# Six low-word roundings go to VectorE, w_in's fourths are converted ahead of w_out's, and the issue order is ranked anew

## The chip, the cores and the metric

The kernel runs on one core of one Trainium2 chip. The metric is the device time in microseconds of one execution. The profile calls the engines PE (TensorE), DVE (VectorE), ACT (ScalarE), POOL (GpSimd) and SP (SyncE, which issues the transfers); PEld is TensorE's weight load.

## The reference, cut to what matters

Three stages follow one another. `x` is 8 x 8 x 512 x 64 and `state` 8 x 8 x 32 x 64; the mixture stages see 4352 tokens of 512 columns. The weights `w_in` and `w_out` reach the kernel as 64-bit floats, so each element is a low and a high 32-bit word.

```python
def attn(x, state):                        # both directions of attention
    a = softmax(scale * x @ state.T);  xread = a @ state
    a2 = softmax(scale * state @ x.T); sread = a2 @ x
    return concatenate([xread, sread], axis=2)
def moe(x, w_in, w_out):                   # 512 -> 2048 -> 512
    h = x @ w_in
    return (h * sigmoid(h)) @ w_out
def moe2(x, phi, w1, w2):                  # 32 slots, 8 experts
    logits = x @ phi
    slots = softmax(logits, axis=0).T @ x
    slot_out = per expert: relu(slots @ w1) @ w2
    return softmax(logits, axis=1) @ slot_out
```

## The kernel before

The tokens are worked through in nine blocks: blocks 0 to 7 hold the 512 read tokens of one batch entry each, block 8 the 256 state tokens. A block does the attention of its batch entry, then 16 hidden tiles `h` (`hid`, 128 hidden columns each): six full-array matmuls on split (high and low part) operands into one PSUM bank, an activation into a tile `g` (six buffers), a VectorE transpose into `blk`. The tiles of one fourth of the hidden columns use one product `wb` of the state with a fourth of `w_in`, made by `wb_mm` with tiled matmuls `wbp` and then split by a ScalarE copy (high part) and a VectorE or GpSimd subtraction (low part). `logits` multiplies `g` by `w2p`, which is w_out times phi, one fourth at a time; until it has run, the `g` buffers stay in use. `s_rep` and `s_dTg` are the softmax over tokens and the slot sums `S`.

Ahead of this, and beside block 0, the two 64-bit weights are turned into fp32. Each comes as four fourths in two halves, 16 halves of 1024 KB in all (`raw`). `conv` (line 546) does one half in four steps: ScalarE's Prelu pass on the high words (`win<-raw` or `acc<-raw` in the profile); ScalarE's Identity pass, which scales and rounds the low words to integers (`part<-raw,ulps`); VectorE's shift of the first result by 3 bits (`win<-win`, `acc<-acc`); GpSimd's integer addition of the two (`win<-win,part`, `acc<-acc,part`). The halves go in the order w_in, w_in, w_out, w_out for each fourth (line 532). A finished w_in fourth lets its `wbp` run; a finished w_out fourth goes through `w2ps` (matmul), a copy `w2s`, `w2q` (matmul) and a copy into `w2p`. Eight raw halves fit in two buffers; a later load is issued when a half has been converted. In blocks 1 to 6 `conv_nat` (line 556) converts w_out once more in another layout; its two-input VectorE operation `blk<-blk` reads the strided low words too.

In block 0 the softmax of the first batch entry stands in front of the first `h`: scores `sc` in PSUM, ScalarE's copy `e`, VectorE's transposes `s`, reductions (`tm`, `asm`), a subtraction, `a_soft1` to `a_soft3`, and the split `ar`, whose low part VectorE computes for this entry.

The order of the instructions on each engine is not that of the code. A recorder (`Recorder`, line 124) collects all operations; its `schedule` plays them through with a cost for each and picks, for the engine that can go first, the ready operation with the smallest rank. The rank is the operation's number in the code, plus `nc.shift`, plus an entry of the table `RANK` (line 48) by zone ("0" is block 0 and what stands ahead of it, "m" blocks 1 to 6, then "7" and "8"), engine, operation, name and count. `LOOK` is how far ahead in time an engine looks for a better candidate. `STAY` and `KEEP` say how much worse a rank may be so that TensorE goes on with full-array work (`STAY`) or tiled work (`KEEP`):

```python
near = [c for c in cands if (c[1].mode == FULL) == (mode == FULL)]
if near:
    near = min(near, key=lambda c: (c[1].prio + SAME * (change(c[1]) > 0.2), c[0]))
    if near[1].prio <= pick[1].prio + (STAY if mode == FULL else KEEP):
        pick = near
```

At the end stand the expert weights `w1` and `w2` (32 MB as loads from `in_w_dram` into `place`, `blk` and `acc`, each issued once its place is free), the slot products `sia`, `sib`, `f`, `so`, and the output tiles `o`.

All compute instructions are recorded on one line of the kernel (427, in `issue`), so the rows are told apart by their tiles.

Of the kernel before, what the change touches and what calls it, by code (L numbers as in the profile page):

```python
# [8 lines left out]
F32R = mybir.dt.float32r  # L9
U32 = mybir.dt.uint32  # L10
# [15 lines left out]

BY_PE = (NB,)

WIN = (2, 6)
WIN8 = (0, 2)  # L30

# [14 lines left out]


RANK = {
    ("0", "ACT", "activation", "acc", 0): 8,
    ("0", "ACT", "activation", "part", 12): 8,  # L50
    ("0", "ACT", "activation", "win", 3): 13,
    ("0", "ACT", "copy", "wb", 2): 71,
    ("0", "DVE", "tensor_scalar", "acc", 0): -9,
    ("0", "DVE", "tensor_scalar", "asm", 3): 120,
    ("0", "DVE", "tensor_tensor", "wb", 0): 459,
    ("0", "DVE", "tensor_tensor", "wb", 3): 126,
    ("0", "DVE", "transpose", "blk", 7): -36,
    ("0", "DVE", "transpose", "s", 4): -40,
    ("0", "PE", "matmul", "lg", 5): 58,
    ("0", "PE", "matmul", "lg", 7): -81,  # L60
    ("0", "PE", "matmul", "wq", 3): -125,
    ("0", "PE", "transpose", "eT", 2): 59,
    ("0", "PE", "transpose", "srT", 1): -75,
    ("7", "DVE", "tensor_reduce", "m", 0): 434,
    ("7", "PE", "matmul", "h", 0): -39,
    ("7", "PE", "matmul", "h", 8): -120,
    ("7", "PE", "matmul", "lg", 5): 30,
    ("7", "PE", "matmul", "wbp", 1): 76,
    ("8", "DVE", "scalar_tensor_tensor", "fin", 0): 68,
    ("8", "PE", "matmul", "S", 3): 155,  # L70
    ("8", "PE", "matmul", "f", 9): 165,
    ("8", "PE", "matmul", "f", 13): 120,
    ("8", "PE", "matmul", "h", 17): 166,
    ("8", "PE", "matmul", "lg", 6): 120,
    ("8", "PE", "matmul", "so", 4): 51,
    ("8", "PE", "transpose", "gt", 8): 71,
    ("8", "PE", "transpose", "hT", 3): -134,
    ("8", "PE", "transpose", "lT", 0): 120,
    ("m", "ACT", "activation", "m", 0): 698,
    ("m", "DVE", "tensor_scalar", "asm", 1): 28,  # L80
    ("m", "PE", "matmul", "S", 2): -150,
    ("m", "PE", "matmul", "h", 5): -324,
    ("m", "PE", "matmul", "lg", 8): -96,
    ("m", "PE", "matmul", "lg", 9): -50,
    ("m", "PE", "transpose", "lT", 0): 416,
}


# [35 lines left out]
class Recorder:  # L124
# [90 lines left out]
    def cost(self, op, eng, what, outs, ins, kwargs):  # L215

        def n(v):
            r = 1
            for s, c in list(v.ap)[1:]:
                r *= c  # L220
            return r

        ps = bass.MemoryType.PSUM
        most = max(n(v) for v in outs + ins)
        pin, pout = any(v.space == ps for v in ins), any(v.space == ps for v in outs)
        strided = any(list(v.ap)[-1][0] > 1 and list(v.ap)[-1][1] > 1 for v in outs + ins)
        if eng == PE:
            lhs, rhs = kwargs.get("lhsT"), kwargs.get("rhs")
            if what == "transpose":
                op.mode, op.tail = FULL, 0.2  # L230
                op.cost += 0.11
                return
            rows, cols = list(lhs.ap)[0][1], n(lhs)
            op.mode = (128 if rows > 64 else 64 if rows > 32 else 32, 128 if cols > 64 else 64 if cols > 32 else 32)
            N = n(rhs)
            if op.mode == FULL:
                split = rhs.dtype == F32R
                op.cost += N / 2.4e3 + 0.0212 if split else max(0.2, 4 * N / 2.4e3 + (0.021 if N > 256 else 0.04))
                op.tail = 0.165
            else:  # L240
                tiles = (128 // op.mode[0]) * (128 // op.mode[1])
                m = 2 * len(op.calls)
                op.cost = max(m / tiles * 2 * N / 2.4e3, m * 0.0135) + (0.07 if tiles == 16 else 0.0068 * tiles)
                op.tail = 0.165
        elif eng == ACT:
            f = kwargs.get("func")
            base = 0.833e-3 * most
            if f in (AF.Abs, AF.Sign, AF.Relu):
                lat = base + (0.26 if pin else 0.29)
            elif len(ins) > 1 and most < 1024:  # L250
                lat = base + (0.258 if pin else 0.285)
            else:
                lat = base + (0.16 if pin else 0.205)
            if kwargs.get("accum_out") is not None:
                op.cost, op.tail = lat + 0.096, 0.0
            else:
                op.cost, op.tail = lat - 0.105, 0.105
            op.mode = {AF.Exp: "e", AF.Silu: "s", AF.Tanh: "es"}.get(f)
        elif eng == DVE:
            sb = [kwargs[x] for x in ("in0", "in1") if x in kwargs and kwargs[x].space == bass.MemoryType.SB]  # L260
            fast = not pin and not pout and what in ("tensor_scalar", "tensor_copy")
            op.port = len(sb) > 1 or fast
            if what == "transpose":
                lat = 0.165 + most / 0.96e3
            elif what == "reciprocal":
                lat = 0.165 + max(0, most - 4) * 6.7e-3
            elif fast:
                lat = 0.262 + most / 1.92e3
            else:
                lat = (0.205 if pin and len(ins) > 2 else 0.155) + most / 0.96e3  # L270
            op.cost, op.tail = lat - 0.08, 0.0 if fast else 0.08
        elif eng == POOL:
            lat = 0.2 + most * 2.135e-3
            if most == 1024:
                lat = 2.39 if outs[0].dtype == F32R else 1.94
# [26 lines left out]
    def schedule(self):  # L302
# [37 lines left out]
        while n_left:  # L340
            best = None
            for e in avail:
# [110 lines left out]
        return lambda *a, **k: self._rec.record(self._eng, what, call, a, k)  # L453


LOOK = {PE: 0, DVE: 0.302, ACT: 0.098, POOL: 0.05, SP: 0.0}
DMA_RATE = 405e3
FULL = (128, 128)
STAY, KEEP, SAME = 60, 60, 30


@with_exitstack
def tile_state_attention_soft_moe(
# [91 lines left out]

# [21 lines left out]
    def share(half):  # L577
        return part[:, 2 * half:2 * half + 2]

    def wo_half(fq, half):  # L580

        n = 4 * fq + 2 + half
        conv(raw_at(n), acc[:, 2 * half:2 * half + 2], share(half))
        if n >= 4:
            next_raw()
        if half == 0:
# [11 lines left out]
        nc.scalar.mul(out=w2p[:, fq].rearrange("p i s -> p (i s)"), in_=p[:, 0:128], mul=-0.5)  # L598

    def win_half(fq, half):  # L600
        n = 4 * fq + half
        conv(raw_at(n), win_t[fq][:, :, 256 * half:256 * half + 256], share(half))
        if n >= 4:
            next_raw()

# [49 lines left out]
    def a_split(b):  # L655
# [506 lines left out]
    for k in range(NB):  # L1162
# [4 lines left out]
        for j in range(16):  # L1167
# [107 lines left out]
    p = s_dTg(NB)  # L1275
# [177 lines left out]
```

## Time and profile before

| what | us |
|---|---|
| median of 3 runs (467.29 to 468.88) | 467.94 |
| the profiled execution | 466.55 |
| its span | 464.0 |
| PE busy in the span | 414.1 (89%) |
| DVE busy | 296.3 (64%) |
| ACT busy | 279.6 (60%) |
| POOL busy | 135.5 (29%) |

The span runs from the first to the last instruction of the profiled execution; that execution's own time is 2.55 us longer. A row of the timeline gives start, duration, engine, operation, output and inputs, and in brackets how long the engine was idle before and what ended that. The chain of waits follows the end of the kernel back to what released it at each step.

### The profile page before, as it was taken

To read this page: it belongs to the slowest core of one execution; us is meant where nothing else is said; L and a number is where in the kernel's file an instruction comes from. 1 tells how busy PE (TensorE), PEld (TensorE's weight loads), DVE (VectorE), ACT (ScalarE), POOL (GpSimd) and SP (SyncE) were. 2 spreads that over 40 slices of the span, in tenths; PEclk is the share of its full clock that TensorE was granted. 3 is DMA by queue.
4 is the path that set the end of the run, shared out by engine and by line. 5 is a ranking of instruction groups with operands and counts; after the bars stand their busy time and mean duration, and the time that the engine had idled before them with its cause. 6 is when DMAs were issued, how large, how long until landed. Compare 5 with 4: busy or idle time off the path is not lost.

```text
span 464.0 us, 12243 instructions
## 1 busy us (share of the span) xinstructions
PE 414.1 (89%) x5334; PEld 261.6 (56%) x5334; DVE 296.3 (64%) x519; ACT 279.6 (60%) x488; POOL 135.5 (29%) x75
## 2 busy tenths in 40 slices
PE   1177789999999999999999999999999998899870
PEld 0044456667757766865775776676476784334420
DVE  0876774797787797789778778779942424221280
ACT  3799998758586495585757759568457413011170
POOL 2464577224124133222412313421056410000000
PEclk9999999999999999999999999999999999899995
DMA  8998740510602412142060251212385899999898
GB/s 317 425 429 330 297 167 1 184 59 35 229 2 92 150 80 93 54 175 93 1 229 1 92 171 59 93 47 93 131 324 182 311 375 420 398 426 424 324 331 305
DMA packets 19845, 92.20 MB, mean 199 GB/s; under 512 B 1616, under 2 KB 5072, under 8 KB 11344
## 3 DMA queue, kind: packets, MB, share of 16 engines
q1 hardware_dynamic: 19792, 91.43, 51.3%
q8 instruction: 41, 0.67, 0.6%
q14 instruction: 12, 0.10, 0.1%
HBM read 79.37 MB, written 12.06 MB: 197 GB/s over the span
## 4 chain that ended last, share of the span: by engine, by line
PE 78%; ACT 7%; DMA 6%; DVE 3%; POOL 2%; issue 1%; SPq 0%; DVEq 0%; POOLq 0%
PE h L427 41%; PE S L427 8%; PE lg L427 7%; PE wbp L427 6%; DMA place<-in_w_dram 4%; PE f L427 3%; PE sc L427 2%; ACT part L427 2%; DMA xT<-in_xT_dram 2%; PE eT L427 2%; PE sr L427 2%; PE o L427 1%; PE sib L427 1%; POOL win L427 1%; PE dT L427 1%
## 5 line engine op out<-in xcount | busy, mean ns | idle before, releaser
L427 PE MATMUL h<-ar,wb 128*128 128x512 f32 x768 | 190.2, 400 | 2.0 <-ACT g L427 2.0
L427 PEld LDWEIGHTS h<-ar,wb 128*128 128x128 f32 x768 | 141.7, 190 | 41.3 <-issue 6.9
L427 DVE STREAM_TRANSPOSE blk<-g 128x512 f32<-128x512 f32 x128 | 86.4, 693 | 39.1 <-ACT g L427 38.9
L427 ACT ACTIVATE g<-h 128x512 f32<-128x512 f32 x100 | 59.3, 602 | 77.9 <-PE h L427 56.8
L427 POOL TENSOR_TENSOR wb<-wf,wb 128x512 fp32r<-128x512 f32 x28 | 36.6, 1307 | 152.4 <-ACT wf L427 90.2
L427 PE MATMUL wbp<-win,ss 64*32 64x512 f32 x512 | 34.0, 610 | 10.0 <-POOL win L427 10.0
L427 PEld LDWEIGHTS lg<-g,w2p 128*32 128x32 f32 x1152 | 29.1, 109 | 18.9 <-issue 5.7
L427 ACT CAST wb<-wbp 128x512 fp32r<-128x512 f32 x64 | 34.7, 604 | 7.2 <-PE wbp L427 7.2
L427 PE MATMUL lg<-g,w2p 128*32 128x128 f32 x1152 | 39.0, 276 | 0.0
L427 PE MATMUL S<-blk,dT 32*32 32x512 f32 (+1 forms) x1040 | 38.5, 598 | 0.4 <-ACT dT L427 0.4
L427 POOL TENSOR_TENSOR s<-s,tm 128x1024 f32<-128x1024 f32 x12 | 23.3, 1939 | 33.4 <-DVE tm L427 33.4
L427 DVE TENSOR_TENSOR wb<-wbp,wb 128x512 fp32r<-128x512 f32 x36 | 24.3, 681 | 6.4 <-ACT wb L427 6.3
L427 ACT ACT_TABLE_LOAD x21 | 26.9, 1283 | 1.1 <-PEq L1443 0.7
L427 POOL TENSOR_TENSOR win<-win,part 128x1024 uint32<-128x1024 uint32 x8 | 19.4, 2436 | 24.9 <-DVE win L427 8.6
L427 POOL TENSOR_TENSOR wlo<-win,whi 128x1024 fp32r<-128x1024 f32 x8 | 18.9, 2389 | 16.5 <-ACT whi L427 16.5
L427 POOL TENSOR_TENSOR acc<-acc,part 128x1024 uint32<-128x1024 uint32 x8 | 20.5, 2559 | 9.3 <-ACT part L427 4.6
L427 DVE SCALAR_TENSOR_TENSOR g<-thb,h 128x512 f32<-128x512 f32 x28 | 18.2, 677 | 5.7 <-ACT thb L427 5.7
L427 PEld LDWEIGHTS wbp<-win,ss 64*32 64x32 f32 x512 | 7.5, 106 | 24.8 <-POOL win L427 11.8
L427 PE MATMUL h<-whi,rd 128*128 128x512 f32 x64 | 20.7, 404 | 0.0
L427 PEld LDWEIGHTS S<-blk,dT 32*32 32x32 f32 (+1 forms) x1040 | 13.0, 103 | 13.2 <-issue 8.6
L427 DVE SCALAR_TENSOR_TENSOR acc<-acc,m,S 128x512 f32<-128x512 f32 x28 | 19.1, 742 | 2.0 <-PE S L427 2.0
L427 ACT ACTIVATE part<-raw,ulps 128x1024 uint32<-128x1024 uint32 x16 | 20.0, 1256 | 0.0
(151 smaller groups left out, 563.7 us busy)
## 6 DMA issues: line engine op xcount, KB each, us to landing
place<-in_w_dram SPq DMA_DIRECT2D x17, 1024.0 KB, 9.4
blk<-in_w_dram SPq DMA_DIRECT2D x13, 1024.0 KB, 10.0
raw<-in_w_in_dram SPq DMA_DIRECT2D x8, 1024.0 KB, 7.8
xT<-in_xT_dram SPq DMA_DIRECT2D x8, 1024.0 KB, 5.2
raw<-in_w_outT_dram SPq DMA_DIRECT2D x8, 1024.0 KB, 7.8
xk<-in_xk_dram SPq DMA_DIRECT2D x8, 1024.0 KB, 5.0
blk<-in_w_out_dram SPq DMA_DIRECT2D x6, 1024.0 KB, 4.8
wo_f<-blk SPq DMA_DIRECT2D x6, 512.0 KB, 2.7
```

Of the source, the lines that this page charges most:

```text
L427: made = [call(*args, **kwargs) for call, args, kwargs in op.calls]
```

## The change

`conv` takes a flag: for six of the 16 halves, the first half of each fourth from the fifth half on, the low words are scaled and rounded by one VectorE operation instead of ScalarE's Identity pass. The fourths are taken in the order of `RAW`: w_in 0 and 1, w_out 0, w_in 2, w_out 1, w_in 3, w_out 2 and 3; the loads, the calls and the lookup of a half's place follow it. The first entry's transposes read PSUM instead of the copy `e`. `RANK`, `LOOK`, `STAY`, `KEEP` and several costs of the planner have new values; equal ranks are settled by the operation's number.

```diff
+RAW = [("win", 0), ("win", 1), ("wo", 0), ("win", 2), ("wo", 1), ("win", 3), ("wo", 2), ("wo", 3)]
+LOW_DVE = (4, 6, 8, 10, 12, 14)
...
+    ("0", "DVE", "tensor_scalar", "win", 3): 404,
...
+    ("0", "DVE", "transpose", "s", 1): 394,
...
+    ("0", "SP", "dma_start", "cst", 0): 112,
+    ("0", "SP", "dma_start", "phi", 0): 451,
+    ("0", "SP", "dma_start", "raw", 2): -6,
+    ("0", "SP", "dma_start", "raw", 4): 190,
+    ("0", "SP", "dma_start", "raw", 6): 131,
+    ("0", "SP", "dma_start", "raw", 7): 253,
+    ("0", "SP", "dma_start", "ss", 1): 265,
...
-            fast = not pin and not pout and what in ("tensor_scalar", "tensor_copy")
+            fast = not pin and not pout and not strided and what in ("tensor_scalar", "tensor_copy")
...
-LOOK = {PE: 0, DVE: 0.302, ACT: 0.098, POOL: 0.05, SP: 0.0}
+LOOK = {PE: 0, DVE: 0.05, ACT: 0.05, POOL: 0.05, SP: 0.0}
...
-STAY, KEEP, SAME = 60, 60, 30
+STAY, KEEP, SAME = 403, 479, 30
...
-    halves = [(kind, f, x) for f in range(4) for kind in ("win", "wo") for x in range(2)]
+    halves = [(kind, f, x) for kind, f in RAW for x in range(2)]
...
-    def conv(raw, dst, r):
+    def conv(raw, dst, r, low):
...
-        nc.scalar.activation(out=r, in_=lo, func=AF.Identity, scale=2.0**-29, bias=ulps)
+        if low:
+            nc.vector.tensor_scalar(out=r, in0=lo, scalar1=2.0**-29, scalar2=2.0**23, op0=ALU.mult, op1=ALU.add)
+        else:
+            nc.scalar.activation(out=r, in_=lo, func=AF.Identity, scale=2.0**-29, bias=ulps)
...
-            nc.vector.transpose(out=s[:, 0, h2, :], in_=e[:, 0, h2, :])
+            nc.vector.transpose(out=s[:, 0, h2, :], in_=e[:, 0, h2, :] if b else p[h2])
...
     wb(0)
+    win_half(1, 0)
     a_soft2(0)
+    win_half(1, 1)
     a_soft3(0)
-    wo_half(0, 0)
-    wo_half(0, 1)
...
             if k == 0 and i == 0 and fq < 3:
-                win_half(fq + 1, 0)
-                win_half(fq + 1, 1)
-                wo_half(fq + 1, 0)
-                wo_half(fq + 1, 1)
+                for kind, f in RAW[2 * fq + 2:2 * fq + 4]:
+                    for half in range(2):
+                        (win_half if kind == "win" else wo_half)(f, half)
```

The table `RANK` had 37 entries and has 78; of them those are shown that the prediction speaks of.

## Rows read from the trace of the kernel before

**Rows 1.** Stretches: span, busy us (instructions) by engine, PE clock, DMA share, GB/s

```profile
0.00:29.68 29.68, 7.69 (x40) 0.87 (x40) 17.25 (x23) 18.86 (x22) 10.59 (x9) 1.00 0.94 384
29.68:70.00 40.32, 33.10 (x318) 21.59 (x324) 28.36 (x42) 39.45 (x54) 24.93 (x11) 1.00 0.74 283
...
70.00:380.00 310.00, 309.98 (x3974) 210.55 (x3959) 225.09 (x395) 202.02 (x371) 99.96 (x57) 1.00 0.33 122
129.76:168.12 38.36, 38.36 (x518) 26.05 (x511) 30.30 (x54) 25.86 (x51) 11.42 (x7) 1.00 0.27 98
```

**Rows 2.** Waits in 0 to 130 us: total us, times, longest

```profile
PE wbp L427 <- POOL win L427: 10.0, 2, 8.8
...
PE w2ps L427 <- POOL acc L427: 4.2, 2, 2.4
```

**Rows 3.** Chain of waits, 0 to 130 us: start, us, what

```profile
63.10 1.15 ACT part L427
...
66.67 2.38 POOL win L427
69.10 1.95 PE wbp L427 x32
```

**Rows 4.** Instructions in order of time, ahead of the first h: start, us, what

```profile
17.34 2.37 POOL L427 TENSOR_TENSOR win<-win,part 128x1024 uint32<-128x1024 uint32 x1 [7.05 <-DVE asm L427]
...
18.97 0.78 DVE L427 TENSOR_SCALAR tm<-tm 128x32 f32<-128x32 f32 x1
...
25.42 2.36 POOL L427 TENSOR_TENSOR acc<-acc,part 128x1024 uint32<-128x1024 uint32 x1 [1.41 <-DVE acc L427]
...
25.96 2.90 DVE L427 TENSOR_TENSOR ar<-s,ar 128x1024 fp32r<-128x1024 f32 x1
...
27.83 1.92 PE L427 MATMUL w2ps<-acc,phi 128*32 128x512 f32 x4 [1.84 <-POOL acc L427]
```

**Rows 5.** Groups by operation and shape, 0 to 130 us: busy, mean ns, idle

```profile
L427 ACT ACTIVATE part<-raw,ulps 128x1024 uint32<-128x1024 uint32 x16 | 20.0, 1256 | 0.0
...
L427 DVE TENSOR_SCALAR acc<-acc 128x1024 uint32<-128x1024 uint32 x8 | 5.5, 690 | 0.2 <-ACT acc L427 0.2
...
L427 DVE STREAM_TRANSPOSE s<-e 128x512 f32<-128x512 f32 x8 | 5.4, 696 | 5.2 <-ACT e L427 5.2
L427 DVE TENSOR_TENSOR s<-s,tm 128x1024 f32<-128x1024 f32 x4 | 4.9, 1221 | 0.1
...
L427 DVE SCALAR_TENSOR_TENSOR blk<-blk 128x1024 f32<-128x1024 uint32 x1 | 1.2, 1178 | 0.0
```

**Rows 6.** In order of time: two readers of one bank, a transpose out of PSUM

```profile
84.19 0.27 ACT L427 COPY ls<-lg 128x128 f32<-128x128 f32 x1 [0.44 <-PE lg L427]
...
84.49 0.29 DVE L427 TENSOR_REDUCE m<-lg 128x1 f32<-128x128 f32 x1
...
372.71 0.72 DVE L427 STREAM_TRANSPOSE siaTs<-siaT 128x512 f32<-128x512 f32 x1 [5.40 <-PE siaT L427]
```

**Rows 7.** Chain of waits: TensorE's groups after a change of kind and within one

```profile
33.56 1.49 PE h L427 x6
...
71.05 1.01 PE lg L427 x32
...
72.65 1.39 PE h L427 x6
...
106.13 0.57 PE lg L427 x16
```

**Rows 8.** The end: busy time by stretch, then the chain of waits

```profile
395.00:400.00 5.00, 5.00 (x32) 1.04 (x32) 0.74 (x5) 0.69 (x1) 0.00 (x0) 0.70 1.05 426
...
385.89 3.43 PE sia L427 x32
...
394.89 5.21 PE sib L427 x32
...
416.23 20.70 DMA place<-in_w_dram
```

More of the change, by code (lines that the diff above doesn't have):

```diff
@@ L48 @@
 RANK = {
[L49 to L83, printed above, removed]
@@ L84 @@
-    ("m", "PE", "matmul", "lg", 9): -50,
-    ("m", "PE", "transpose", "lT", 0): 416,
+    ("0", "ACT", "activation", "acc", 4): 184,
+    ("0", "ACT", "activation", "e", 3): -52,
+    ("0", "ACT", "activation", "g", 6): 121,
+    ("0", "ACT", "activation", "g", 8): 162,
+    ("0", "ACT", "activation", "g", 9): 298,
+    ("0", "ACT", "activation", "g", 14): 205,
+    ("0", "ACT", "activation", "part", 6): -116,
+    ("0", "ACT", "activation", "win", 6): 46,
+    ("0", "ACT", "activation", "win", 7): -240,
@@ new lines @@
+    ("0", "ACT", "copy", "e", 3): 79,
+    ("0", "ACT", "copy", "wb", 0): 257,
+    ("0", "ACT", "copy", "wb", 1): 201,
+    ("0", "ACT", "copy", "wb", 4): 65,
+    ("0", "ACT", "copy", "ws", 2): 115,
+    ("0", "ACT", "copy", "ws", 3): -366,
+    ("0", "DVE", "reciprocal", "asm", 1): 67,
+    ("0", "DVE", "tensor_scalar", "acc", 3): -86,
+    ("0", "DVE", "tensor_scalar", "asm", 2): -43,
+    ("0", "DVE", "tensor_scalar", "part", 0): 136,
+    ("0", "DVE", "tensor_scalar", "part", 2): 64,
+    ("0", "DVE", "tensor_scalar", "tm", 1): 95,
@@ new lines @@
+    ("0", "DVE", "tensor_scalar", "win", 3): 404,
+    ("0", "DVE", "tensor_tensor", "wb", 2): 101,
+    ("0", "DVE", "transpose", "s", 1): 394,
+    ("0", "DVE", "transpose", "s", 4): -38,
+    ("0", "PE", "matmul", "h", 1): 797,
+    ("0", "PE", "matmul", "lg", 7): -127,
+    ("0", "SP", "dma_start", "cst", 0): 112,
[3 more added lines that the diff above has]
+    ("0", "SP", "dma_start", "raw", 6): 131,
@@ new lines @@
+    ("0", "SP", "dma_start", "raw", 7): 253,
+    ("0", "SP", "dma_start", "ss", 1): 265,
+    ("7", "ACT", "copy", "lg", 0): -202,
+    ("7", "ACT", "copy", "wb", 2): 90,
+    ("7", "DVE", "scalar_tensor_tensor", "wp", 0): -480,
+    ("7", "DVE", "tensor_scalar", "wp", 0): -687,
+    ("7", "PE", "matmul", "h", 6): -478,
+    ("7", "PE", "matmul", "lg", 0): 219,
+    ("7", "PE", "matmul", "lg", 10): -87,
+    ("7", "PE", "matmul", "lg", 14): -341,
+    ("7", "PE", "matmul", "wbp", 0): 114,
+    ("7", "PE", "matmul", "wbp", 2): -369,
@@ new lines @@
+    ("8", "PE", "matmul", "S", 0): -250,
+    ("8", "PE", "matmul", "f", 12): 468,
+    ("8", "PE", "matmul", "f", 15): 747,
+    ("8", "PE", "matmul", "h", 1): 105,
+    ("8", "PE", "matmul", "h", 15): 60,
+    ("8", "PE", "matmul", "o", 1): 112,
+    ("8", "PE", "matmul", "so", 31): -358,
+    ("8", "PE", "matmul", "top", 1): -557,
+    ("8", "PE", "transpose", "gt", 8): 86,
+    ("8", "PE", "transpose", "hT", 0): -38,
+    ("8", "PE", "transpose", "hT", 2): -809,
+    ("8", "PE", "transpose", "hT", 3): -577,
@@ new lines @@
+    ("8", "PE", "transpose", "lT", 0): 216,
+    ("m", "ACT", "activation", "e", 0): 480,
+    ("m", "ACT", "activation", "s", 0): 232,
+    ("m", "ACT", "activation", "sums", 0): 444,
+    ("m", "ACT", "copy", "e", 0): 413,
+    ("m", "ACT", "copy", "wb", 2): 160,
+    ("m", "ACT", "copy", "wf", 1): 208,
+    ("m", "ACT", "copy", "wf", 2): 254,
+    ("m", "DVE", "scalar_tensor_tensor", "blk", 0): -716,
+    ("m", "DVE", "tensor_scalar", "blk", 1): -159,
+    ("m", "DVE", "tensor_tensor", "blk", 0): -1300,
@@ L86 @@
+    ("m", "DVE", "transpose", "blk", 9): 23,
+    ("m", "PE", "matmul", "S", 0): -697,
+    ("m", "PE", "matmul", "h", 2): -360,
+    ("m", "PE", "matmul", "h", 6): -504,
+    ("m", "PE", "matmul", "h", 8): -640,
+    ("m", "PE", "matmul", "lg", 8): -39,
+    ("m", "PE", "matmul", "sr", 0): -491,
+    ("m", "PE", "matmul", "wbp", 2): -378,
+    ("m", "PE", "transpose", "eT", 1): 380,
+    ("m", "PE", "transpose", "lT", 0): -117,
+    ("m", "PE", "transpose", "srT", 0): 250,
 }
@@ L249, in cost @@
                 lat = base + (0.26 if pin else 0.29)
-            elif len(ins) > 1 and most < 1024:
+            elif most == 1024 and outs[0].dtype == U32:
+                lat = 1.256
+            elif f == AF.Prelu:
+                lat = 1.165
+            elif len(ins) > 1:
                 lat = base + (0.258 if pin else 0.285)
@@ L580, in wo_half @@
     def wo_half(fq, half):
-        n = 4 * fq + 2 + half
-        conv(raw_at(n), acc[:, 2 * half:2 * half + 2], share(half))
+        n = halves.index(("wo", fq, half))
+        conv(raw_at(n), acc[:, 2 * half:2 * half + 2], share(half), n in LOW_DVE)
         if n >= 4:
@@ L600, in win_half @@
     def win_half(fq, half):
-        n = 4 * fq + half
-        conv(raw_at(n), win_t[fq][:, :, 256 * half:256 * half + 256], share(half))
+        n = halves.index(("win", fq, half))
+        conv(raw_at(n), win_t[fq][:, :, 256 * half:256 * half + 256], share(half), n in LOW_DVE)
         if n >= 4:
```

10 lines of the change are left out of this document (5 added, 5 removed).

## The prediction

> **What bounds the kernel now.** I read the busy times by stretch first [rows 1]. From 70 to 380 us TensorE is busy in 309.98 of 310.00 us, and one block of the main loop (129.76 to 168.12) is 38.36 us of TensorE without a gap. There the other engines set nothing, and only TensorE's own work counts. All that can be won on waits lies ahead of 70 us: 7.69 us busy in the first 29.68, then 33.10 of 40.32, so 7.2 us of idle in this second stretch. In it ScalarE is busy 39.45 us (98%), VectorE 28.36 (70%), GpSimd 24.93.
>
> The waits of the first 130 us come second [rows 2]: TensorE waits 10.0 us in wbp for w_in (POOL win), 8.8 of them once, behind the add that ends at 19.71 us [rows 4], and 4.2 us in w2ps for w_out (POOL acc). The rest of its idle is the first transfer, which the change leaves in its place in the queue.
>
> The chain of waits third [rows 3]: the last w_in fourth is added only at 66.67 to 69.05, TensorE waits for it, and its wbp starts at 69.10. From there the chain is TensorE alone. ScalarE sets when: the chain comes out of its part pass at 63.10 to 64.25 us, and each half needs two passes of this engine, which is 98% busy.
>
> Last, the instructions ahead of the first h [rows 4]. ar (VectorE) takes 2.90 us from 25.96 and GpSimd's add runs from 25.42 to 27.78; the same two-input form of 1024 columns takes 1.22 us elsewhere [rows 5]. So ar stands until the add ends. The small tm operation at 18.97 ends at 19.75, just after an add ended at 19.71. Both show VectorE held by a running GpSimd add. Then TensorE ends a w2ps group (27.83, 1.92 us) before the first h can go, at 29.75.
>
> **The change part by part.** *Six low words.* ScalarE loses six passes of 1.256 us [rows 5]; back to back one stands in the chain with 1.15 [rows 3], so I take 6 x 1.15 = 6.9 us. VectorE gains six operations on 1024 columns, read with a step of two words. The trace has no such operation with one input. The nearest rows [rows 5]: the two-input operation on the same strided low words, 1.178 us, and the one-input shift on packed words, 0.690 us. I take 1.18, because the read pattern is the same: 6 x 1.18 = 7.1 us; the lower end is 6 x 0.69 = 4.1. The first of the six is the fifth half, so all fall behind about 25 us.
>
> Here a rule speaks otherwise. The Trainium skill (VectorE: DVE Perf Modes, What auto-detection actually checks) gives a one-input 32-bit operation between SBUF operands two elements a cycle and asks only that the outermost dimension be even, which this pattern is whatever its step. By that the six would cost about the packed shift's 0.69, and the sum would be that of the first rival; no row of before shows which.
>
> *The stretch from 29.68 to 70 us.* ScalarE falls to 39.45 - 6.9 = 32.6 us, VectorE rises to 28.36 + 7.1 = 35.5, TensorE needs 33.1. The longest is then VectorE: 40.3 - 35.5 = 4.8 us less at best, and I take 4.5, since VectorE won't run without any idle. Ends: 7.2 (TensorE's whole idle, if block transposes slide past 70 us) and 0.
>
> *w_in ahead of w_out.* The work per half is the same (two passes, shift, add). The last w_in half moves from place 14 to 12 of 16; at (69.05 - 19.71)/12 = 4.1 us a half (second to fourteenth half) that is some 8 us earlier, so the wait of [rows 3] goes. What is late next is w_out: logits need w2p, and while they wait the six g buffers fill. The last w_out half stays in place 16, and behind its add come w2ps, w2q and two copies; this cost is inside the ends above, and the second rival is its price. Raw loads change their order on SP; a load of 1.05 MB at the 384 GB/s of [rows 1] is 2.7 us, and I cost this at nothing since ScalarE, 98% busy, covers it. If the cover goes, it is 2.7 us a place. The SP queue's new ranks (phi, constants, the rest of the state, raw 4, 6 and 7 put back) fall under the same cover.
>
> *Ahead of the first h.* With two w_in halves in the place of the two w_out halves, w2ps no longer stands in front of h: 29.75 - 28.86 = 0.9 us. The second half's shift there gets rank +404, so its add no longer overlaps ar: 2.90 - 1.22 = 1.7; and the shift itself (0.69 [rows 5]) leaves the path. Together 3.3 us. Another add may meet ar instead, so I take 2.0; ends 3.3 and -1.2 (one more 1024-column operation ahead of ar).
>
> *Transposes of block 0 out of PSUM.* They read the bank that ScalarE's copy reads. In [rows 6] VectorE's m, which takes nothing from ls, starts 0.04 us after ScalarE's ls on the same bank ends (84.19 + 0.27). So such reads are put in order, the transposes start no earlier, and this edit costs nothing. Nor does the second one's rank of +394, by which other ready VectorE work of this path goes first; a transpose of this size out of PSUM takes 0.72 us [rows 6] against 0.70 out of SBUF [rows 5].
>
> *Ranks, LOOK, STAY, KEEP.* They order TensorE's full-array and tiled work. A trip to tiled work and back costs, from [rows 7]: lg x32 is 1.01 and lg x16 0.57, so 0.44 for each 16 and 0.13 over; the first six h after a change 1.49 against 1.39, 0.10 more. That is 0.23 a trip; a block has some five. The larger STAY and KEEP keep one kind longer. I take 0.5 us (two trips in all) and one trip in each of six blocks either way, 1.4, as ends.
>
> *The tail.* The transfers fill the DMA engines (a share of 1.05 from 395 to 400 us) [rows 8], and the chain ends in a weight that landed at 436.93. The loads wait for buffers that TensorE frees, so all moves with it. I take 0. Ends of 1.5 both ways: sib takes 5.21 us at a mean granted clock of 0.70 (395 to 400 us; part of it at the lower level, 1.2 GHz) where sia, as large, takes 3.43 [rows 8].
>
> Sum: 2.0 + 4.5 + 0.5 = 7.0 us. The profiled execution took 466.55 us, 464.0 of it the span; 457.0 + 2.55 = 459.6. The median, 467.94, is 1.4 above that execution, so I forecast 460.9 for the median.
>
> **The rivals.**
>
> *The rounding is fast.* At 0.69 VectorE has 28.36 + 4.1 = 32.5 us, below TensorE's 33.1, and the stretch loses all 7.2: 9.7 in all, 458.2. For: the packed shift. Against: the strided row at 1.178. Only if GpSimd's adds don't hold it.
>
> *Another wait takes the cover.* w2p comes so late that the g buffers fill, or VectorE's backlog delays the low parts of wb, and the stretch keeps its 40.3 us; only 2.5 us are left, 465.4. For: the first six h take 6 x 1.39 = 8.3 us and then need w2p of a w_out fourth that is now behind w_in. Against: in the same stretch TensorE also has scores, wbp and eT to do.
>
> *The tail keeps its end.* If the weight stream starts no earlier, the end stands and the time is 467.9. For: the DMA engines are full there [rows 8]. Against: those loads wait for TensorE.
>
> *Slower: the adds hold the roundings.* GpSimd runs 24.93 of 40.32 us [rows 1]. If the new operation is of the kind that a running add holds, as tm and ar were, each can lose ar's 1.68 us: 6 x (1.18 + 1.68) = 17.2 us on VectorE, which has 40.32 - 28.36 = 12.0 free. It decides from 12.0/6 = 2.0 us an operation; at 2.86 the stretch grows by 5.2, and less the 2.0 in front the time is 471.1. Against: it has one input and a strided read, and no row shows such a one held. The Trainium skill (GPSIMD Engine Reference, Specifications) names as those that contend VectorE's instructions in a two-port mode or with two SBUF inputs; by it this rival needs the fast form of the first one.
>
> **How the numbers follow.** Forecast 0.43, fast rounding 0.20, another wait 0.17, tail 0.07, slower 0.13. A measurement of this kernel tells 0.3%, 1.4 us, from no change. Faster: 0.43 + 0.20 + 0.17 = 0.80; same 0.07; slower 0.13. Downwards the range takes the fast rounding with all ends (3.3 + 7.2 + 1.4 + 1.5 = 13.4: 454.5), upwards the two cases that lose the gain, 465.4 and 467.9 with about half a microsecond over; what lies above 468.4 is the slower rival's.
>
> **What would show it.** Right: 10 part passes on ScalarE and 6 on VectorE of about 1.18 us; the first h near 27.7 us; TensorE without a wait of over 1 us for POOL win behind the first wbp; TensorE's idle between the first h and 65 us at 2 to 3 us; blocks of 38.1 to 38.4 us; the end of the weights 7 us earlier. Wrong: roundings of over 2 us that end with GpSimd's adds, h waiting for ACT g behind w2ps or w2q, first h later than 29.7, or weights that land at 437 again.

## The result and the profile after

The changed kernel takes 464.19 us (median of 4 runs, 463.13 to 464.67) where the kernel before took 468.41 beside it (467.29 to 469.04): ratio 0.9899, 95% interval 0.9864 to 0.9935. A second timing, six runs on one chip, gave 464.17 and a ratio of 0.9907 (0.9881 to 0.9934). The forecast was 460.9, with a range of 454.5 to 468.4 and a chance of 0.80 for faster. The sign and the range hold; the likeliest value is 3.3 us too low. The profiled execution took 463.13 us with a span of 460.5, so 3.5 us of span are gained where the sum had 7.0.

First the busy time by stretch, with the columns of [rows 1]; the fourth line is one block of the main loop, the fifth the start of the hidden tiles, the last the slot product sib.

```profile
0.00:29.68 29.68, 6.21 (x41) 1.81 (x41) 15.56 (x24) 19.76 (x24) 10.51 (x9) 0.98 0.94 383
29.68:70.00 40.32, 37.75 (x350) 23.77 (x351) 35.85 (x48) 36.49 (x53) 27.50 (x11) 0.88 0.72 286
70.00:380.00 310.00, 308.84 (x3938) 207.23 (x3937) 225.35 (x396) 200.64 (x366) 99.46 (x57) 1.00 0.34 125
128.07:166.69 38.62, 38.62 (x519) 25.37 (x511) 30.14 (x54) 26.24 (x50) 11.50 (x8) 1.00 0.27 96
28.00:36.00 8.00, 6.85 (x76) 4.98 (x77) 6.68 (x8) 7.18 (x8) 3.57 (x2) 0.57 1.01 391
...
392.00:398.00 6.00, 4.80 (x68) 1.81 (x68) 2.05 (x8) 0.69 (x1) 0.00 (x0) 1.00 1.03 384
```

From 29.68 to 70 us TensorE's idle fell from 7.22 to 2.57 us, ScalarE from 39.45 to 36.49 busy, VectorE rose from 28.36 to 35.85. Part of TensorE's busy time is work at the lower level of its clock (1.2 GHz): the granted clock from 28 to 36 us is 0.57. The block takes 38.62 us in place of 38.36.

Where the 3.5 us are is read from milestones of TensorE's timeline: dT of block n (the step ahead of a block's slot sums), the starts of sia and siT, and sib's duration in the chain of waits. All in us.

| kernel | time | dT 0 | dT 1 | dT 5 | sia | sib takes | siT | span |
|---|---|---|---|---|---|---|---|---|
| before | 466.55 | 91.39 | 129.76 | 283.16 | 385.71 | 5.21 | 401.00 | 464.0 |
| after | 463.13 | 90.69 | 128.07 | 282.46 | 384.19 | 3.69 | 397.82 | 460.5 |
| difference | -3.42 | -0.70 | -1.69 | -0.70 | -1.52 | -1.52 | -3.18 | -3.5 |

So up to dT 1 the kernel gains 1.7; over the next four blocks it gives 1.0 back; blocks 6 to 8 bring 0.8, sia to siT 1.7, the rest 0.3. Two things limit this reading. dT 0 is not the same point of the work in both: before has issued 120 matmuls of h ahead of it, after 126; ahead of dT 1, dT 5 and sia the counts of every kind agree. And a second profile of the changed kernel (from the second timing, span 461.6) has dT 0 at 91.69, dT 1 at 129.07, dT 5 at 283.48, sia at 385.20 and siT at 398.84: behind dT 1 the same to 0.1 us, but the gain up to dT 1 is then 0.7.

The groups by operation, 0 to 130 us, and TensorE's waits in the same stretch:

```profile
L476 ACT ACTIVATE part<-raw,ulps 128x1024 uint32<-128x1024 uint32 x10 | 12.4, 1244 | 1.0 <-POOL win L476 0.9
L476 DVE TENSOR_SCALAR part<-raw 128x1024 uint32<-128x1024 uint32 x6 | 10.0, 1668 | 0.0
...
L476 DVE STREAM_TRANSPOSE s<-sc 128x512 f32<-128x512 f32 x2 | 1.4, 708 | 3.2 <-ACT e L476 3.2
```

```profile
PE sc L476 <- DMA xT<-in_xT_dram: 11.5, 1, 11.5
PE wbp L476 <- POOL win L476: 8.7, 2, 8.3
PE h L476 <- ACT ar L476: 2.3, 1, 2.3
PE h L476 <- DVE wb L476: 1.8, 1, 1.8
PE wbp L476 <- ACT wf L476: 1.2, 1, 1.2
PE h L476 <- DVE ar L476: 0.7, 1, 0.7
PE eT L476 <- ACT e L476: 0.7, 1, 0.7
```

The last long wait for w_in [rows 3] is gone, and no w2ps waits for POOL acc: of the waits of [rows 2] only the first, 8.3 us long, is left. The two transposes out of PSUM take 0.71 us each, the first from the end of ScalarE's copy on. The mean of VectorE's six roundings hides two kinds. In order of time, with GpSimd's adds:

```profile
29.64 2.89 POOL L476 TENSOR_TENSOR acc<-acc,part 128x1024 uint32<-128x1024 uint32 x1 [2.75 <-ACT part L476]
30.19 2.88 DVE L476 TENSOR_SCALAR part<-raw 128x1024 uint32<-128x1024 uint32 x1
...
45.85 3.23 POOL L476 TENSOR_TENSOR acc<-acc,part 128x1024 uint32<-128x1024 uint32 x1 [2.37 <-DVE acc L476]
47.95 1.67 DVE L476 TENSOR_SCALAR part<-raw 128x1024 uint32<-128x1024 uint32 x1
50.38 2.75 POOL L476 TENSOR_TENSOR acc<-acc,part 128x1024 uint32<-128x1024 uint32 x1 [1.30 <-DVE acc L476]
53.37 0.65 DVE L476 TENSOR_SCALAR part<-raw 128x1024 uint32<-128x1024 uint32 x1
53.79 2.51 POOL L476 TENSOR_TENSOR win<-win,part 128x1024 uint32<-128x1024 uint32 x1 [0.65 <-ACT part L476]
60.03 2.41 POOL L476 TENSOR_TENSOR acc<-acc,part 128x1024 uint32<-128x1024 uint32 x1 [0.70 <-ACT g L476]
60.67 2.32 DVE L476 TENSOR_SCALAR part<-raw 128x1024 uint32<-128x1024 uint32 x1
```

Where no add runs, a rounding takes 0.65 us (the sixth 0.68). Where one runs, the rounding ends 0.54 to 0.57 us after it in all four cases (29.64 + 2.89 = 32.53, and 30.19 + 2.88 = 33.07). It waits for the add and then does its 0.6 us: 10.0 us in all, of which about 6 are waiting.

Ahead of the first complete h:

```profile
11.54 1.96 PE L476 MATMUL sc<-xT,ss 64*32 64x512 f32 x16 [11.54 <-DMA xT<-in_xT_dram]
18.58 3.21 POOL L476 TENSOR_TENSOR win<-win,part 128x1024 uint32<-128x1024 uint32 x1 [4.54 <-DVE win L476]
21.84 1.96 PE L476 MATMUL wbp<-win,ss 64*32 64x512 f32 x16 [8.34 <-POOL win L476]
28.45 1.22 DVE L476 TENSOR_TENSOR ar<-s,ar 128x1024 fp32r<-128x1024 f32 x1
28.47 0.58 PE L476 MATMUL h<-ar,wb 128*128 128x512 f32 x1 [2.28 <-ACT ar L476]
29.73 2.50 PE L476 MATMUL h<-ar,wb 128*128 128x512 f32 x5 [0.68 <-DVE ar L476]
32.16 1.94 PE L476 MATMUL sr<-xk,e 128*32 128x64 f32 x64
```

ar is free of the adds, 1.22 us where it took 2.90 [rows 4]. But the first scores start at 11.54, 2.5 us later than the 9.00 of before, because a half of w_in now precedes the first xT on SP. wbp is 2.1 us later, and five sixths of the first h start at 29.73, where all six started at 29.68.

### The profile page after: what moved, and what is told of

The parts are those of the page before. It is cut to its first block, busy times and chain, and to the rows that moved or that the text cites. A ratio compares the mean times of both kernels' runs of the same rounds, so it can differ in the third digit from the quotient of the medians.

```text
span 460.5 us, 12251 instructions
## 1 busy us (share of the span) xinstructions
PE 412.9 (90%) x5334; PEld 259.9 (56%) x5334; DVE 302.0 (66%) x525; ACT 275.8 (60%) x482; POOL 137.5 (30%) x75
## 4 chain that ended last, share of the span: by engine, by line
PE 79%; DMA 6%; ACT 5%; DVE 4%; POOL 1%; issue 1%; SPq 0%; DVEq 0%; POOLq 0%
PE h L476 43%; PE lg L476 8%; PE S L476 7%; PE wbp L476 6%; DMA place<-in_w_dram 4%; PE f L476 3%; DMA xT<-in_xT_dram 2%; PE sr L476 2%; PE sc L476 2%; PE eT L476 2%; PE o L476 1%; PE dT L476 1%; ACT e L476 1%; DVE place L476 1%; PE sib L476 1%
## 5 line engine op out<-in xcount | busy, mean ns | idle before, releaser
L476 PE MATMUL h<-ar,wb 128*128 128x512 f32 x768 | 194.0, 405 | 5.1 <-ACT ar L476 2.3
L476 PE MATMUL lg<-g,w2p 128*32 128x128 f32 x1152 | 41.8, 276 | 0.0
L476 POOL TENSOR_TENSOR ar<-s,ar 128x1024 fp32r<-128x1024 f32 x7 | 16.8, 2399 | 19.3 <-ACT ar L476 19.3
L476 ACT COPY e<-eT 128x512 f32<-128x512 f32 x16 | 9.6, 602 | 18.2 <-PE eT L476 18.2
L476 DVE TENSOR_REDUCE tm<-s 128x32 f32<-128x1024 f32 x16 | 19.3, 1207 | 1.1 <-ACT s L476 1.1
```

The lines of the kernel that those rows point to most:

```text
L476: made = [call(*args, **kwargs) for call, args, kwargs in op.calls]
```

## The experiments

Experiments 1 to 9 are single runs. Before took 469.52 us in a single run beside 1 to 4, 469.08 beside 5, 6, 7 and 9; its eleven runs beside 8 and 10 have spans of 464.0 to 467.6 us, so its one profile here, 464.0, is at their fast end. The changed kernel's ten runs have spans of 460.5 to 462.5.

Two profiles of one kernel differ at dT 0 by 1.0 us (the changed kernel) and 1.6 us (that of experiment 9: 90.07 and 88.47), and rows name the difference, the granted clock. In one profile of each pair it was down at the lower level (0.50 from 80.9 to 84.3 us, 0.51 from 79.3 to 82.8), and 18 matmuls of h took 5.95 and 5.96 us in place of 4.38. The same matmuls stand ahead of dT 1 in before, after and experiments 1 to 8. So up to there two things can be told apart: idle time is waiting, and a difference in busy time is mostly the level of the clock. TensorE up to dT 1, in us:

| kernel | dT 1 | idle | busy |
|---|---|---|---|
| before | 129.76 | 29.21 | 100.55 |
| after | 128.07 | 27.21 | 100.86 |
| after, second profile | 129.07 | 28.36 | 100.71 |
| 1 | 133.69 | 27.91 | 105.78 |
| 2 | 131.53 | 29.46 | 102.07 |
| 3 | 131.65 | 27.49 | 104.16 |
| 4 | 128.79 | 28.46 | 100.33 |
| 5 | 131.36 | 28.99 | 102.37 |
| 6 | 130.44 | 27.63 | 102.81 |
| 7 | 132.24 | 29.69 | 102.55 |
| 8 | 128.26 | 27.13 | 101.13 |

**1. One rank undone: raw 2.**

```diff
-    ("0", "SP", "dma_start", "raw", 2): -6,
```

> The changed kernel without the rank of -6 on raw 2, planned again: the load of w_in 1's first half stands behind the first xT again. Theory (that load, put ahead of xT, cost the first scores 2.5 us): the first scores start at 9.0 us in place of 11.54, the first full h group 1.5 to 2.5 us earlier than 29.73, and the span is 458 to 460 us. Rival (the first h hangs on VectorE's chain and the following stretch on ScalarE, whatever lands first): the scores start earlier, but the first block's dT stays at 128 us and the span at 460.5 or above.

Measured 471.74 us, span 469.2. sc came at 9.33 and wbp at 19.65, as the theory has it, but the complete first h later, at 30.73. The planner made a different order from the one missing entry (sr and srT went ahead of h), and dT 1 came at 133.69. Of the 5.6 us to after, 0.7 are idle and 4.9 busy time for the same matmuls: this run spent longer at the lower level (granted clock 0.51 from 44.8 to 51.7 us). The run says that this entry carries the order around it; it does not price xT's place. From here on orders were frozen where one part was to be changed.

**2. After's order, the six roundings back on ScalarE.** The order is planned as in the changed kernel; then the six operations are issued on the other engine.

```diff
+        for op, eng, call, args, kwargs in self.swaps:
+            op.eng, op.calls = eng, [(call, args, kwargs)]
```

> The changed kernel's order as it stands, with the six roundings put back on ScalarE at their places. Theory (ScalarE is full from 40 to 60 us, so six passes of 1.15 us back on it delay TensorE): TensorE's idle between the first h and 80 us grows from 3.7 us by 2 to 4, and the span becomes 462.5 to 465. Rival (the roundings, 10.0 us on VectorE with what GpSimd's adds hold them, cost there what they save): span within 1 us of 460.5, or lower.

Measured 467.23 us, span 464.7: dT 1 at 131.53 (+3.5 us), the blocks as in after, sib 3.69.

```profile
29.68:70.00 40.32, 34.12 (x300) 21.49 (x304) 23.91 (x38) 38.02 (x52) 25.24 (x10) 0.96 0.72 282
```

TensorE's busy time falls back from 37.75 to 34.12 us and ScalarE's rises to 38.02 of 40.32. The matmuls of h wait for ScalarE's g, 4.7 us in all, where after's two profiles have 0.4 and 1.3:

```profile
PE h L478 <- ACT g L478: 4.7, 2, 4.1
```

Against after's two profiles dT 1 is 2.5 to 3.5 us later, 1.1 to 2.3 of it idle and the rest clock; against the spans of after's ten runs this one is 2.2 to 4.2 longer. So in this order the low words on VectorE are worth that much, nearly all by dT 1. Without them the run lies among before's (464.7, before 464.0 to 467.6).

**3. Before's order, the six roundings on VectorE.** The same swap the other way round.

```diff
+        if n in (4, 6, 8, 10, 12, 14):
+            nc.swaps.append((op, DVE, tc.nc.vector.tensor_scalar, (), dict(
+                out=r, in0=lo, scalar1=2.0**-29, scalar2=2.0**23, op0=ALU.mult, op1=ALU.add)))
```

> The order of before as it stands, with the fifth, seventh, ninth, eleventh, thirteenth and fifteenth half's rounding on VectorE at their places. Theory (the low words alone bring a good part): each rounding takes about 0.66 us when no add of GpSimd runs and otherwise ends about 0.55 us after the add; TensorE's idle between 29.7 and 70 us falls from 7.2 to 3 to 5, span 460 to 462. Rival (the order brought the gain, the low words nothing): span 463.5 or more.

Measured 468.48 us, span 465.7, dT 1 at 131.65 (before 129.76). ScalarE was relieved (12.4 us of part passes in place of 20.0), and the roundings cost as much as in after:

```profile
L429 DVE TENSOR_SCALAR part<-raw 128x1024 uint32<-128x1024 uint32 x6 | 9.4, 1565 | 1.1 <-POOL win L429 1.1
```

The waits did fall: TensorE idled 27.49 us up to dT 1, 1.7 less than in before and as little as in after. Still dT 1 came later, since its busy time for the same matmuls is 3.6 us more: the time came back as clock (0.60 granted from 48 to 54 us, where before shows 1.00). So neither half of the change shows a gain in time alone, but the low words take waits away in either order. Whether this order would keep its 3.6 us at the lower level in a second profile was not tried.

**4. Before's ranks for blocks 1 to 8 behind after's front.** The table has before's entries for the zones "m", "7" and "8", and before's 60 holds there for STAY and KEEP.

```diff
-                        if near[1].prio <= pick[1].prio + (STAY if mode == FULL else KEEP):
+                        if near[1].prio <= pick[1].prio + ((60 if pick[1].late else STAY) if mode == FULL else (60 if pick[1].late else KEEP)):
```

> The changed kernel's ranks for block 0 and what stands ahead, with the ranks and the limits STAY and KEEP of before for the later blocks. Theory (the new ranks make each block of the main loop 0.24 us longer): blocks of 38.35 us in place of 38.60, 1.4 us less by the end of block 6; with the old end's sib at the lower clock 1.5 us of it is lost again, so the span is 459 to 461. Rival (the block's length comes from how block 0 leaves the engines, not from these ranks): blocks stay at 38.6.

Measured 466.26 us, span 463.5. The blocks return to 38.35 us, so the new ranks of the middle cost 0.25 us a block. dT 0 to dT 1 takes 39.15 us where after takes 37.38, but most of that is the milestone: here, as in before, 120 matmuls of h stand ahead of dT 0, and six more take about 1.5 us (an estimate from 18 in 4.38). dT 1, where the work is the same, comes at 128.79, between after's two profiles, and at dT 5 the two kernels stand 0.3 us apart, less than one kernel's spread. What this run loses, it loses at the end: dT 5 to sia takes 102.92 us (after 101.73), and sib took 5.38 again, so that sia to siT took 15.71 (after 13.63). That is 3.3 us, about the whole difference to after. With the new ranks of blocks 7 and 8 kept (experiment 6) the two pieces take 102.02 and 13.64, so those ranks, with their limits, carry most of it.

**5. All of before's ranks and limits, with the new RAW and roundings.** RANK is before's whole table.

```diff
-LOOK = {PE: 0, DVE: 0.05, ACT: 0.05, POOL: 0.05, SP: 0.0}
+LOOK = {PE: 0, DVE: 0.302, ACT: 0.098, POOL: 0.05, SP: 0.0}
...
-STAY, KEEP, SAME = 403, 479, 30
+STAY, KEEP, SAME = 60, 60, 30
```

> After with the table RANK, LOOK, STAY and KEEP of before (RAW and the six roundings stay); the planner makes a new order from them. Theory (the new ranks carry part of the gain, in the stretch ahead of 80 us and at the end): TensorE's idle from 29.7 to 80 us is 5 us or more (after 3.7), blocks are 38.35, sib runs over 4 us at a lower granted clock again, time 466 to 468. Rival (RAW and the six roundings carry it all): idle under 4 us, dT of block 1 by 128.5, time 464 or less.

Measured 469.24 us, span 466.3: TensorE's idle from 29.7 to 80 us is 6.4 us (after 3.7, in its second profile 5.5), dT 1 at 131.36, blocks 38.33. Up to dT 1 the idle is 0.6 to 1.8 us more than in after's profiles, and 1.5 to 1.7 more are clock. So the theory is weakly borne out in the front: RAW and the roundings without the new ranks show no gain, but half of the difference is not waiting. It fails for the end. sib ran in 3.69 us, although the order there is before's:

```profile
391.70 1.92 PE L435 MATMUL S<-blk,dT 128*32 128x512 f32 x16 [0.35 <-ACT dT L435]
393.56 0.39 PE L435 MATMUL top<-fin,cst 128*128 128x3 f32 x2
395.34 0.67 PE L435 MATMUL sibT<-thb,r4e 64*32 64x128 f32 x32 [1.40 <-DVE fin L435]
```

In after the slot sums S stand in two parts around top, and sibT follows 3.51 us behind the first of them, in place of 3.64:

```profile
388.52 1.06 PE L476 MATMUL S<-blk,dT 128*32 128x512 f32 x8 [0.35 <-ACT dT L476]
389.52 0.39 PE L476 MATMUL top<-fin,cst 128*128 128x3 f32 x2
389.83 1.06 PE L476 MATMUL S<-blk,dT 128*32 128x512 f32 x8
392.03 0.67 PE L476 MATMUL sibT<-thb,r4e 64*32 64x128 f32 x32 [1.13 <-DVE fin L476]
```

With S in one piece sib took 5.2 to 5.4 us at a granted clock of 0.68 to 0.70 in three profiles of four; with S in two parts it took 3.69 in all ten profiles. That agrees with the order as the cause, but it does not show it: the fourth profile has the old order and the full clock.

**6. Before's ranks for blocks 1 to 6 alone.** As 4, but only for the zone "m".

```diff
-            op.late = self.zone != "0"
+            op.late = self.zone == "m"
```

> After with the ranks of before for blocks 1 to 6 and their limits of 60 for a change of kind there; the ranks of blocks 7 and 8 stay the new ones. Theory (the new ranks of the middle cost 0.24 us a block, those of the end bring 3): blocks of 38.35, dT of block 1 to dT of block 5 153.4 us (after 154.4), sib near 3.6, time near 463. Rival (the end's ranks work only behind the middle's): sib over 4 us at a lower granted clock, time 464.5 or more.

Measured 466.77 us, span 464.0, so the theory's sum missed by 3.8. The blocks were 38.34 and sib 3.69 as expected; dT 1 to dT 5 took 153.38 us, 1.0 less than in after. Yet dT 5 came 1.4 us later than in after, and the end was another 1.8 us behind siT's own delay of 1.7. The clock accounts for both. Up to dT 1 TensorE idled 27.63 us, between after's two profiles, but was busy 2.0 us longer (0.51 granted from 49.6 to 56.6 us); behind siT the 120 matmuls of f were busy 14.99 us in place of 13.29 (0.51 granted from 401.2 to 404.7). Together that is 3.7 of the 3.8. So this run doesn't show that the 0.25 us a block can't be had alone; that is open.

**7. The first xT ahead of raw 2, in after's order.**

```diff
+        move(find("SP", "dma_start", "raw", 2), find("SP", "dma_start", "raw", 1))
...
+        move(c2[1], c3[1])
+        move(c2[3], c2[1], c2[2], c1[3])
+        move(c3[2], find("DVE", "tensor_tensor", "ar", 0))
+        move(c3[3], c3[2], c2[3])
```

> After's order, but the first xT and raw 1 go ahead of raw 2 on SP, and the conversion of that half is fitted in later on ScalarE, VectorE and GpSimd; the shift and the add of the fourth half go behind ar. Theory (raw 2 ahead of xT is what ate the 2 us in front of the first h): sc at 9.0 to 9.4 (after 11.54), wbp near 19.7 (21.84), first h near 26.5 (28.47), dT of block 0 and of block 1 some 1.5 to 2 us earlier, time 462. Rival (the stretch behind is set by the conversions and the clock, not by the first h): first h earlier, but dT of block 1 within 0.5 of after's 128.07, time 463 to 464.

Measured 468.69 us, span 466.1. The front did what the theory said: sc 9.08, wbp 19.37, complete h at 27.92, 1.8 us earlier. dT 0 came 4.2 us later, at 94.86 (2.5 of it idle), through the edit itself:

```profile
28.55 2.73 POOL L509 TENSOR_TENSOR win<-win,part 128x1024 uint32<-128x1024 uint32 x1 [3.30 <-DVE win L509]
...
31.32 1.22 ACT L509 ACTIVATE part<-raw,ulps 128x1024 uint32<-128x1024 uint32 x1 [4.71 <-POOL win L509]
```

The next part pass writes the buffer that the delayed add still reads, so ScalarE, the engine that sets the stretch, stood still for 4.71 us.

**8. The same without that wait.** The fourth half's shift stays where it was, and only steps of later halves go behind ar.

```diff
-        move(c3[2], find("DVE", "tensor_tensor", "ar", 0))
-        move(c3[3], c3[2], c2[3])
+        for e, at in late.items():
+            for o in [o for o in order if o.eng == e and any(o in c for c in self.convs[4:])]:
+                if order.index(o) < order.index(late[e]):
+                    move(o, at)
```

> As in the run with xT ahead of raw 2, but no conversion waits for ar: the third half's last two steps go ahead of the fourth half's add, the fourth half's shift keeps its place ahead of the transpose, and only steps of later halves that stood ahead of ar on ScalarE or VectorE go behind it. Theory (that run lost 4 us by the add put behind ar, for which ScalarE stood 4.7 us; the first h itself sets little): sc at 9.1, first h near 27.0 to 27.5, no ScalarE wait of over 2 us for POOL win, dT of block 0 within 1 us of after's 90.69, time 462.5 to 464.5. Rival (what is won in front of the first h reaches the end): dT of block 0 near 89, time near 462.

Measured 464.45 us, span 461.6, dT 0 at 90.88: as after. sc is at 8.82 and wbp at 19.13, yet the complete h starts at 29.63:

```profile
23.49 5.00 POOL L513 TENSOR_TENSOR win<-win,part 128x1024 uint32<-128x1024 uint32 x2 [4.42 <-DVE win L513]
...
26.21 3.36 DVE L513 TENSOR_TENSOR ar<-s,ar 128x1024 fp32r<-128x1024 f32 x1
...
29.63 2.50 PE L513 MATMUL h<-ar,wb 128*128 128x512 f32 x5 [2.60 <-DVE ar L513]
```

The two adds that after has done or spread by then now run from 23.49 to 28.49 and hold ar for 3.36 us. So in the two orders tried an early xT cost as much elsewhere: in 7 at ScalarE, here at ar, which a late xT leaves free of adds, and h starts at 29.6 to 29.7 as in after.

**9. TensorE kept at work ahead of the first h.** warm[0] is the bank of the first logits.

```diff
+    for key, n in ((("matmul", "wbp", 0), 4), (("matmul", "h", 0), 1)):
+        nc.fill[("0", PE) + key] = n * [(tc.nc.tensor.matmul, (warm[0],), dict(
+            lhsT=win_t[0][:, 0, 0:128], rhs=win_t[0][:, 0:2, 0:256], start=True, stop=True))]
```

> After's order, plus five full-array matmuls of w_in with itself into the still unused logits bank: four ahead of wbp, one ahead of the first h; their product is never read. Theory (the first h groups of after run at the lower level of the clock because TensorE idled ahead of them): granted clock 1.00 from the first h on, the five h 1.2 to 1.5 us instead of 2.50, sr near 1.0 instead of 1.87, dT of block 0 some 2 us earlier, time near 462. Rival (the clock does not follow what TensorE did before, or what follows is set by the conversions): h and sr as in after, or dT of block 1 within 0.5 of 128.07, time 463 to 465.

Measured 461.70 us, span 459.6, dT 0 at 90.07, dT 1 at 127.45. The rows of after's first h, in this kernel:

```profile
28.92 1.44 PE L479 MATMUL h<-ar,wb 128*128 128x512 f32 x5 [0.77 <-DVE ar L479]
30.30 1.10 PE L479 MATMUL sr<-xk,e 128*32 128x64 f32 x64
31.33 1.66 PE L479 MATMUL h<-ar,wb 128*128 128x512 f32 x6
```

1.44 for 2.50 us, 1.10 for 1.94, 1.66 for 2.37: 2.6 us in three groups, so in after these ran at the lower level, and work ahead of them lifts it. At dT 0 only 0.6 us of it are left, but not because of the conversions. Up to 65.58 us, where a group sc starts (after: 67.70), 2.1 us are won; then this profile has the lower level from 79.3 to 82.8 us (0.51 granted), where after's has 1.00. The same 18 matmuls, first in after, then here:

```profile
81.40 4.38 PE L476 MATMUL h<-ar,wb 128*128 128x512 f32 x18
...
79.20 5.96 PE L479 MATMUL h<-ar,wb 128*128 128x512 f32 x18
```

Of the second profiles (from 10), it is the changed kernel's that has these slow 18, and there dT 0 is 88.47 against 91.69. Like with like, the gain at dT 0 is 2.2 us without them and 1.6 with them: the theory is right up to there. Behind it the last weight takes part of it back. In the second profile siT starts at 395.59, 2.2 us ahead of after's 397.82, but the weight lands at 432.32, 1.1 ahead of 433.45.

**10. The candidates timed again, beside each other:** the changed kernel, the same with the matmuls of 9, and 8 with them.

> The changed kernel as it is, timed beside the other two on the same chip: near 464, ratio near 0.990 if the first timing holds.

> The changed kernel with the five extra matmuls alone, timed in five rounds. Theory (they bring 0.6 us by dT of block 0 and keep it to the end): 1 to 2 us under the changed kernel's own time in the same call, ratio to the kernel before 0.985 to 0.987. Rival (the one look was a good draw): as the changed kernel.

> The same with the five extra matmuls that keep TensorE at work ahead of the first h. Theory (conversions on ScalarE set the stretch once the clock is up): dT of block 0 near 90.0, as with the matmuls alone, time 461 to 462.5. Rival (both gains add up): dT of block 0 near 88.5, time 460 or less.

| kernel | median (6 runs) | range | ratio to before (95%) |
|---|---|---|---|
| before (11 runs) | 468.70 | 466.54 to 470.28 | |
| after | 464.17 | 463.39 to 465.34 | 0.9907 (0.9881 to 0.9934) |
| with the five matmuls | 463.06 | 461.39 to 464.24 | 0.9873 (0.9845 to 0.9902) |
| with them and xT first | 463.60 | 462.46 to 463.84 | 0.9885 (0.9858 to 0.9912) |

The matmuls take 1.1 us off the median, at the lower end of what was expected, and the intervals overlap: a likely gain, not a certain one. The two edits do not add up. With xT first the last five sixths of the first h waited 2.92 us for ar, and although the first sixth had run at the upper level in 0.49 us, they took 2.50 again.

## Why the prediction was right, and where its size was off

**What bounds the kernel: right for the front, with two gaps.** Experiment 2 shows ScalarE's passes as what set the stretch that [rows 1] marked. But "the rest of its idle is the first transfer" leaves out 6.0 us: of before's 29.21 us of idle, xT (9.0), wbp (10.0) and w2ps (4.2) are 23.2, and the rest are waits for g, w2s, ss, e and srs inside the stretch, which [rows 2] leaves out. And behind 70 us, where the other engines were to set nothing, the changed kernel waits for wf, 1.2 us in either profile.

**Six low words: both rivals were true, the likeliest case was not.** The forecast had 1.18 us each, 7.1 in all, from the two-input row of [rows 5]. No rounding took 1.18. Alone it takes 0.65 us, which is the first rival's price: the rule that was set against the row there (the Trainium skill, VectorE: DVE Perf Modes, What auto-detection actually checks) is the one that this trace bears out. And in this form a running add holds it, which is the slower rival's mechanism; the Trainium skill (GPSIMD Engine Reference, Specifications) names the same form as one that contends, and the trace agrees with 2.88 us for 0.65. The sum, 10.0 us, is between the forecast's 7.1 and that rival's 17.2, under the 12.0 us that VectorE had free, so it did not decide. The step that failed is the choice of the row: packed and strided one-input reads cost the same, and the second input was what made the STT row dear (the packed two-input row of [rows 5] has 1.22 too). That an add holds a one-input operation could be read in before, in a packed shift of 0.69 us:

```profile
29.61 2.39 POOL L427 TENSOR_TENSOR win<-win,part 128x1024 uint32<-128x1024 uint32 x1 [1.83 <-DVE win L427]
31.48 1.06 DVE L427 TENSOR_SCALAR win<-win 128x1024 uint32<-128x1024 uint32 x1 [2.02 <-ACT win L427]
```

It ends 0.54 us behind the add, so the rival's chance of 0.13 was low for its mechanism, if not for its time.

**The stretch: 4.5 us forecast, 1.7 measured at dT 1** with the front included (0.7 in the second profile). TensorE's idle from 29.68 to 70 us did fall by 4.65 us (2.8 in the second profile), but its idle up to dT 1 only by 2.0 (0.9). The step that failed took the idle of one window for time won: new waits stand outside it or in place of the old ones. xT comes 2.5 us later, eT and the first h wait 3.6 us in all for ScalarE and VectorE, an h waits 1.8 for wb, and at 78.3 us wbp waits 1.2 for wf. The lower clock is not what ate the difference, although experiment 9 shows 2.6 us of it in after's first groups: before's busy time up to dT 1 is within 0.3 us of after's, and its own first h ran at that level too (2.93 us where six at the upper level take 1.65):

```profile
29.68 2.93 PE L427 MATMUL h<-ar,wb 128*128 128x512 f32 x6
```

**Ahead of the first h: 2.0 forecast, nothing measured.** Three of its parts happened: w2ps left the path, ar is unheld, the named shift is behind ar (another, of acc, stands there under ScalarE's half of ar). What cancelled them is in the text as a cover: "the first transfer, which the change leaves in its place in the queue", and raw loads at nothing because ScalarE covers them, else 2.7 us a place. The -6 of raw 2 was in the diff, and it put one load ahead of xT, which nothing covers: 2.54 us at sc, close to the price named. Experiment 8 adds that undoing it wins nothing in the order that it tried.

**Ranks: 0.5 forecast.** The blocks lost 1.0 over four, and at 38.62 they are outside the 38.1 to 38.4 named as a sign; blocks 6 to 8 won 0.8. On balance 0.2 lost, within the ends of 1.4. The step that failed is that there would be fewer trips in the blocks. Counted in the timelines, dT 1 to dT 5 has 31 changes between full-array and tiled work in both kernels, while changes between any two shapes rose from 47 to 63; from dT 5 to sia the former fell from 27 to 21, three trips fewer. (What the new ranks of block 0 did stands in the front's 1.7 and was not taken apart.)

**The tail: taken as 0, with ends of 1.5.** It brought 2.0: sib at 3.69 us in place of 5.21, which is the end that was named, and 0.5 beside it. The chain of the end, sib and the last weight:

```profile
393.24 3.69 PE sib L476 x32
...
414.15 19.30 DMA place<-in_w_dram
```

The weight lands at 433.45 in place of 436.93 [rows 8]: its transfer starts 2.1 us earlier and takes 1.4 less (19.30 for 20.70; why stays open). The span ends 27.0 us behind the landing in both kernels, so the end moved with it, and the rival in which the tail keeps its end is out.

**The transposes out of PSUM: right.** They waited for ScalarE's copy on the same bank, and the first starts 2.60 us behind sc in both kernels: the edit cost nothing.

In sum: -1.7 (-0.7 in the second profile) by the route that was costed at 6.5, +0.2 by the ranks behind it, -2.0 by a tail that was taken as 0. More than half of the gain in span came from a term with no forecast but its ends, and what set sib's clock is open, so that the time came as near to the forecast as 3.3 us is in part luck.

## What to carry to other kernels

Price a moved operation with its new engine's neighbours running: here 0.65 us alone became 1.67 on average, and the whole difference was waiting for another engine's adds. Read every negative rank of a load as a place taken from the load behind it, and ask whether that one is covered. Book idle time as a gain only up to a point that has the same work behind it in both kernels: here one window lost 4.65 us of idle, and the milestone behind it gained 1.7 or 0.7. Take waits and clock apart there, since two profiles of one kernel differed by 2.7 us in busy time for the same matmuls (experiment 9). In a list-scheduled kernel, test a part in a frozen order, since replanning after one changed entry moved the time by more than the whole change did.

## What the runs showed of the hardware

A one-input VectorE operation on 1024 words read with a step of two took 0.65 to 0.68 us, no more than the packed shift's 0.69. Where it or the shift began under a running GpSimd add, it ended 0.54 to 0.61 us behind the add, and the two-input ar 1.08 (before, after in both profiles, and experiment 8): ar took 1.22 us alone, 2.90 under one add [rows 4], 3.36 under two in a row. It works both ways: the add at 29.64 took 2.89 us where one alone takes 2.36, behind a shift that VectorE ran from 29.59 to 30.28.

In the run of the last table row TensorE came to the first h at the upper level (0.49 us for its first matmul, 0.79 without the extra work), waited 2.92 us for ar, and ran the other five in 2.50 us, as slowly as in after; with a wait of 0.77 us they took 1.44. Up to about 33 us the clock column of several profiles shows 1.00 where the durations show the lower level: there is no record that early, and the durations are the better witness. So it is in before, whose [rows 1] show 1.00 from 29.68 us on beside the 2.93 us of its first h.
